# Head-pair loads of B and C turned by VectorE in a chunked scan with a bilinear feed-forward layer

## The chip, the cores and the metric

The kernel runs on one core of a Trainium2 chip. The metric is the device time of one execution in microseconds (us); the median of three runs of the kernel before is 124.91 us (124.63 to 125.03). The core's engines each work through their own list of instructions in order: TensorE (PE in the profile; PEld are its weight loads), VectorE (DVE), ScalarE (ACT), GpSimd (POOL) and SyncE (SP), which here only issues DMAs. SP, ACT and POOL each issue DMAs from their own queue.

## The reference

The inputs are `x` (4 batches, 8 heads, 768 tokens, 32 channels), decays `a` (4, 8, 768), `B` and `C` (4, 8, 768, 16) and three weight matrices, all float32. Per batch and head a linear recurrence is run in chunks:

```python
cum = np.cumsum(log(a)); L = exp(cum_i - cum_j) * causal
y_intra = (C @ B.T * L) @ x                  # inside the chunk
y_inter = (C @ state) * exp(cum)             # from the chunks before
state   = exp(cum_last) * state + sum_j exp(cum_last - cum_j) * B_j x_j
```

Its output, with the 8 heads side by side (3072 rows of 256), goes through `(y @ W_a) * (y @ W_b) @ W_out`, with an inner width of 1536. The result is 3072 x 256 float32.

## The kernel before, in words

The 768 tokens are cut into 6 blocks of 128 tokens, and the 4 batches into 2 pairs of batches, so there are 12 "pairs" p = 2 * block + batch pair. Pairs 0 to 3 (blocks 0 and 1) have an early path of their own, in which two tokens share a partition row. The change leaves that path alone, but for the order of some steps. For pairs 4 to 11 the steps are:

- **Loads.** `loads_bc(p)` issues one DMA for C and one for B of the pair (`load2`, line 163): a partition is a token, and its 256 numbers are 2 batches x 8 heads x 16. So each of the 2048 runs of a DMA is 64 bytes long. `loads_x` does the same for x, with runs of 128 bytes. Nearly all go through SP's queue.
- **Factors.** The decays are scanned on VectorE (`scan`) with the 32 batch-head rows on partitions. `late_rows` (line 276, POOL) divides blocks 2 to 5 by their middle value, into `Ps`; `late_factors` (line 282) turns `Ps` with four 32-row VectorE transposes, so that tokens are on partitions (`fCl`); `fb(k)` takes the reciprocal of one block (`fBl`).
- **Scaling.** `scale_bc` (line 307, POOL) multiplies the loaded B and C with these factors and writes fp16 tiles `bm` and `cm`. `scale_x` (POOL or ScalarE) writes `x16`. `prep(p)` calls the first for C and B.
- **Transposes.** `transposes(p)` (line 323) turns `bm` and `cm` on TensorE, two 128x128 pieces each, into one PSUM bank called `tr`. ScalarE copies from there: twice for B (`bt`, once with the even and once with the odd heads zeroed by `par`) and once for C (`ct`, line 355).
- **Scores.** `scores(p)` (line 366) makes 16 products of `bt` and `ct` into the four banks `SC`; `mask` multiplies three of the four with the causal mask on VectorE, and the fourth either on VectorE too or, `by_pool`, by a ScalarE copy to `tmp` and a POOL multiplication. The results are `t1`.
- **Outputs.** `group(blk)` calls `outputs(blk)` (line 512): products of `ct` with the state, of `x16` with `t1`, and the sums for the next state, `DS`. From PSUM the outputs are read in three parts into `XB`: all of batch 0 of each pair by ScalarE, the two halves of batch 1 by VectorE. `state_sums` (VectorE) and `state_spread` (POOL, writing `spair` and `gU`) update the state.
- **Feed-forward.** `unit(p, k)` for pairs 0 to 3 and `bunit(blk, k)` for blocks 2 to 5 make the two up-products into PSUM banks `aps` and `bps`. ScalarE copies `aps` (`evac_a`), VectorE multiplies it with `bps` into `hk` or `hkb`. `out_half` and `bout` make the down-product into a bank `ops`, which ScalarE copies out and SP stores.

The order on every engine is written out by hand: the calls at the end of the kernel (lines 757 to 1049) are issued in program order, so that block k's scan steps lie between the feed-forward units of block k - 1. Four PSUM banks serve `aps`, `bps`, `ops` and `tr` by turns; which one a product takes is a digit of the string `BANKS` (line 22), and it waits until the bank's last reader is done.

Of the kernel before, what the change touches and what calls it, by code (L numbers as in the profile page):

```python
# [10 lines left out]
f32 = mybir.dt.float32  # L11
# [10 lines left out]
BANKS = (  # L22
    "1301302130213023120312031023120312031203210230123012302103210320132013210231023103201231"
    "0231023102301320132013201321032103210321032103210321032130213021302130213021302130213021"
    "3021302"
)
# [3 lines left out]
def kernel(  # L30
# [26 lines left out]
    NG = NBLK - 1  # L57
    P0 = 4


# [30 lines left out]
    XB = big.tile([128, NBLK - P0 // NBP, 2, 2, NBP, Q], f16, name="XB")  # L91
    U32 = big.tile([128, NP, 2, 2 * D], f32, name="U32")
    gU = big.tile([128, NP, 2, 2 * D], f32, name="gU")
    maskbd = big.tile([128, H, D], f16, name="maskbd")
# [11 lines left out]
    fBl = big.tile([128, NL, NBP * 2 * H], f32, name="fBl")  # L106
    fCl = big.tile([128, NL, NBP * 2 * H], f32, name="fCl")
    hr = big.tile([BH, NG], f32, name="hr")
    hs = big.tile([BH, NG], f32, name="hs")
# [8 lines left out]
    outp = ctx.enter_context(tc.tile_pool(name="outp", bufs=2 * P0 + 2))  # L118
    ps4 = ctx.enter_context(tc.tile_pool(name="ps4", bufs=1, space=PSUM))
    psf = ctx.enter_context(tc.tile_pool(name="psf", bufs=1, space=PSUM))  # L120

# [13 lines left out]


    def tiles(p):
        Bn = inp.tile([128, H, 2, N], f32, name="bn", tag="bn")
        Cn = inp.tile([128, H, 2, N], f32, name="cn", tag="cn")
        Xn = inp.tile([128, H, 2, D], f32, name="xn", tag="xn")  # L140
        pair_in[p] = (Bn, Cn, Xn)
# [17 lines left out]
    def load2(eng, p, which):  # L159
        if p < P0:  # L160
            return [load1(eng, p, which, bt) for bt in range(2)]
        blk, bp = divmod(p, NBP)
        return eng.dma_start(
            by_token(pair_in[p][which]).rearrange("p t h n -> p (t h) n"),
            (B, C, x)[which][2 * bp : 2 * bp + 2, :, blk * Q : (blk + 1) * Q, :].rearrange("t h q n -> q (t h) n"),
        )

    def load_w(W, t, f=None):
# [32 lines left out]
    nc.vector.memset(causal_q, 1.0)  # L201
    nc.vector.memset(c32, 0.0)
    x1 = load1(nc.sync, 1, 2, 0)
    nc.sync.dma_start(c32[0:BH], p32_t.ap())
# [71 lines left out]
    def late_rows(eng):  # L276
# [3 lines left out]
        )  # L280

    def late_factors():
        for c0 in range(0, Q, 32):
            nc.vector.transpose(fCl[c0 : c0 + 32], Ps[:, :, c0 : c0 + 32])

    st = {}
# [20 lines left out]
    def scale_bc(p, which, eng, factor=None):  # L307
        blk, bp = divmod(p, NBP)
        name = ("bm", "cm")[which]
        if p >= P0:  # L310
            f = (fBl, fCl)[which][:, blk - P0 // NBP].rearrange("p (b t h) -> p b t h", b=NBP, t=2)[:, bp]
        else:
            f = (f_c(blk) if which else fB[:, blk])[:, :, bp]
        raw = by_token(pair_in[p][which]) if p >= P0 else pair_in[p][which].rearrange("p h r n -> p r h n")
        m_ = pre.tile([128, 2, H, N], f16, name=name, tag=name)
        eng.tensor_tensor(
            out=m_,
            in0=raw,
            in1=(f if factor is None else factor).unsqueeze(3).broadcast_to((128, 2, H, N)),
            op=ALU.mult,  # L320
        )
        st.setdefault(p, {})[name] = m_
    def transposes(p, ps=None, between=None, apart=False):
        s = st[p]
        if p >= P0:
            ps = [bank("tr").bitcast(f16)] * 2
            TB, TC = ps[0][:, 0:256], ps[0][:, 256:512]
            on_dve = False
        elif ps is None:
            ps = [bank("tb") if p == 1 else SC[0], SC[1]] if apart else None  # L330
            on_dve = apart
            TB, TC = (TT[:, 0:256], TT[:, 256:512]) if ps is None else [t_.bitcast(f16)[:, 0:256] for t_ in ps]
        else:
            on_dve = True
            TB, TC = [t_.bitcast(f16)[:, 0:256] for t_ in ps]
        BT = mid.tile([128, 2, 2, 2, 64], f16, name="bt", tag="bt")
        CT = mid.tile([128, 2, Q], f16, name="ct", tag="ct")
        b_ = []
# [8 lines left out]

        turn(TB, s["bm"])
        if between:
            between()  # L350
        turn(TC, s["cm"])
        copy_bt(0)
        copy_bt(1)
        if p >= P0:
            nc.scalar.copy(CT.rearrange("p t q -> p (t q)"), TC)
            s["BT"], s["CT"] = BT.rearrange("p e r t i -> p e r (t i)"), CT
            return
# [154 lines left out]
    def outputs(blk):  # L512
# [25 lines left out]
        if blk < NBLK - 1:  # L538
            for p in pairs:
                state_sums(p, (1,))  # L540
        whole, low, high = slice(0, 128), slice(0, 64), slice(64, 128)
        for bt, to, fr in ((0, whole, whole), (1, low, high), (1, high, low)):
            if blk == NBLK - 1:
                for j in range(NBP):
                    o_ = XB[to, blk - P0 // NBP, :, bt, j]
                    i_ = SCt[bt][fr, :, cols[j]]
                    if bt == 0:
                        nc.vector.tensor_scalar(o_, i_, YS / XS, None, ALU.mult)
                    else:
                        nc.scalar.activation(out=o_, in_=i_, func=AF.Copy, scale=YS / XS)  # L550
                continue
            o_ = XB[to, blk - P0 // NBP, :, bt].rearrange("p u j q -> p u (j q)")
            i_ = SCt[bt][fr, :, 0 : NBP * Q]
            if bt == 0:
                nc.scalar.activation(out=o_, in_=i_, func=AF.Copy, scale=YS / XS)
            else:
                nc.vector.tensor_scalar(o_, i_, YS / XS, None, ALU.mult)

# [12 lines left out]
    def state_sums(p, bts=(0, 1)):  # L571
        blk, bp = divmod(p, NBP)
        for bt in bts:
# [4 lines left out]
            else:  # L578
                nc.vector.scalar_tensor_tensor(  # L579
                    out=U32[:, p, bt], in0=ds, scalar=g, op0=ALU.mult, in1=gU[:, p, bt], op1=ALU.add  # L580
                )

    def state_spread(p):
# [17 lines left out]
        if blk + 1 < NG:  # L601
            nc.gpsimd.tensor_tensor(
                out=gU[:, p + NBP],
                in0=U32[:, p],
# [128 lines left out]
    def loads_bc(p, eng=None):  # L733
        if p < NP:
            tiles(p)
            for w in (1, 0):
                load2(eng or nc.sync, p, w)

# [4 lines left out]
    def fb(k):  # L743
        if k * NBP >= P0:
            nc.vector.reciprocal(fBl[:, k - P0 // NBP], fCl[:, k - P0 // NBP])
        else:
# [65 lines left out]
    scan(5, NBLK)  # L812
    over_mid(2, NBLK)
    for w in range(2):
        for bt in range(2):
# [67 lines left out]
    scale_bc(3, 1, nc.gpsimd)  # L883
    late_rows(nc.gpsimd)
    scale_x(3, nc.gpsimd)
    pull(2)
    pv(2)
# [5 lines left out]
    h()  # L893
    late_factors()
    fb(2)
    h = unit(2, 1)

    def prep(p, spread=()):
        if p < NP:
            scale_bc(p, 1, nc.gpsimd)  # L900
            scale_bc(p, 0, nc.gpsimd)
        for q in spread:
# [36 lines left out]

    scores(3)  # L940
    prep(4, (2,))
    loads_x(4, nc.sync)
    for p in range(6, NP):
        loads_bc(p)
        if p < 10:
            loads_x(p - 1, nc.sync)
    mask(product(3, 3), by_pool=True)
    mask(product(3, 0))
# [6 lines left out]
    pull(3)  # L955
    pv(3)
    go((2, 5))
    transposes(4)
    state_sums(3)
    state_spread(3)  # L960
    fb(3)
    out_half(2, 0)
# [3 lines left out]
    scores(4)  # L966
    mask(product(4, 3), by_pool=True)
    prep(6)
    masked(4, (0, 1))
# [3 lines left out]
    mask(product(5, 3), by_pool=True)  # L973
    prep_x(5)
    out_half(2, 1)
# [7 lines left out]
    h()  # L983
    go((3, 5))
    group(2)
    transposes(6)
# [4 lines left out]
    stage(6, True, (4, 5))  # L991
    fb(4)
    prep_x(7)
    masked(6, (0, 1))
    masked(6, (2,), *bu(2, 0, 1, 2))
    scale_x(6, nc.scalar)
    bgo(2, 3, 4)
    stage(7, True)
    fb(5)
    prep(8)  # L1000
    prep(9)
    prep_x(8)
    prep(10)
    for p in range(9, NP):
        loads_x(p)
    masked(7, (0, 1, 2), *bu(2, 5, 6, 7, 8, 9, 10, 11))
    group(3)
    transposes(8)
# [7 lines left out]
    masked(8, (0, 1))  # L1016
    masked(8, (2,), *bu(3, 0, 1, 2, 3, 4, 5))
    for blk in range(4, NBLK):
        pB = blk * NBP + 1
        stage(pB, False)  # L1020
        if blk + 1 < NBLK:
            transposes(pB + 1)
        if blk > 4:
            prep_x(pB)
        masked(pB, (0, 1))
        bout(blk - 2, 2)
        masked(pB, (2, 3), *bu(blk - 1, 6, 7, 8, 9))
        group(blk)
        bout(blk - 2, 3)
        bgo(blk - 1, 10, 11)  # L1030
        if blk + 1 < NBLK:
            stage(pB + 1, False, (pB - 1, pB))
            prep_x(pB + 1)
            masked(pB + 1, (0, 1))
            bout(blk - 1, 0)
            masked(pB + 1, (2,))
            transposes(pB + 2)
            bout(blk - 1, 1)
            masked(pB + 1, (3,), *bu(blk, 0, 1, 2, 3, 4, 5))
    last = NBLK - 1  # L1040
# [39 lines left out]
```

## Time and profile before

| what | value |
|---|---|
| median of the runs | 124.91 us |
| the profiled execution's own time | 125.11 us |
| its span in the profile | 123.4 us |
| PE busy | 117.3 us, 95% |
| DVE busy | 91.0 us, 74% |
| ACT busy | 75.7 us, 61% |
| POOL busy | 61.2 us, 50% |
| SP's queue issuing loads | 21.6 to 59.3 us, without a break |
| q1 (SP's and ScalarE's DMAs): packets, share of 16 DMA engines | 51,808, 36.3% |

The profile is of one execution. Times in its timelines count from the start of the span. A line such as `L342 PE MATMUL tr<-ident,bm ... x16 | 2.2, 221 | 0.0` is a group: source line, engine, operation, written tile and read tiles, shapes, number; then busy us in all, mean ns of one; then the idle time of the engine just before these instructions, and what ended it. Matmuls overlap in a pipeline, so what one adds to the path is read from the starts of its neighbours, not from its own length. The granted TensorE clock was full in this execution.

### The profile page before, as it was taken

How to read it: one execution, taken by the hardware profiler on the slowest of the kernel's cores; microseconds unless marked ns; L12 is line 12 of the kernel's file. 1: busy time of each engine (PE TensorE's matmuls, PEld its weight loads, DVE VectorE, ACT ScalarE, POOL GpSimd, SP SyncE). 2: the span in 40 equal slices, each digit the busy share in tenths (PEclk: the TensorE clock that was granted, in tenths of full speed). 3: DMA queues.
4: the chain of work that ended last, by engine and by line, in shares of the span. 5: the costliest groups of instructions: out<-in, count | busy, mean ns of one | idle time of the engine just before them, and what ended most of it. 6: DMA issues, size and time to landing. Idle time of an engine off the chain costs nothing.

```text
span 123.4 us, 3704 instructions
## 1 busy us (share of the span) xinstructions
PE 117.3 (95%) x1456; PEld 80.0 (65%) x1456; DVE 91.0 (74%) x182; ACT 75.7 (61%) x158; POOL 61.2 (50%) x88
## 2 busy tenths in 40 slices
PE   6799799999999999999999999999999999999990
PEld 2345669889898798744477465757464775555890
DVE  3999598973995979799986988996889544747200
ACT  0447846837669866987669767457637746657220
POOL 7997989099492994097996970056000000000000
PEclk9999999999999999999999999999999999999999
DMA  3999999978899989799977601011101012010122
GB/s 66 195 155 210 185 198 204 164 137 77 89 125 115 108 111 103 91 118 93 129 271 169 204 5 45 5 43 45 43 0 43 5 43 88 0 48 0 43 85 85
DMA packets 56401, 12.15 MB, mean 99 GB/s; under 512 B 51168, under 2 KB 55936, under 8 KB 56384
## 3 DMA queue, kind: packets, MB, share of 16 engines
q1 hardware_dynamic: 51808, 7.43, 36.3%
q0 software_dynamic: 2304, 4.06, 17.4%
q10 hardware_dynamic: 2272, 0.43, 1.8%
q8 instruction: 11, 0.18, 0.6%
q14 instruction: 6, 0.05, 0.1%
HBM read 11.13 MB, written 3.15 MB: 116 GB/s over the span
## 4 chain that ended last, share of the span: by engine, by line
PE 85%; DMA 7%; DVE 5%; issue 1%; ACT 0%; DVEq 0%
PE ops L718 17%; PE aps L693 17%; PE bps L693 16%; PE ops L661 9%; PE aps L615 8%; PE bps L615 7%; DMA Wb<-in_moe_w_b_dram 5%; PE SC L372 2%; PE SC L432 2%; PE tr L342 2%; DMA a_sb<-in_a_dram 2%; DVE hk L646 1%; PE bps L628 1%; PE SC L447 1%; PE SC L522 1%; DVE fC L246 1%
## 5 line engine op out<-in xcount | busy, mean ns | idle before, releaser
L639 ACT COPY asb<-aps 128x512 f32<-128x512 f32 x72 | 41.9, 587 | 16.0 <-PE aps L693 10.4
L703 DVE TENSOR_TENSOR hkb<-bps,asb 128x512 f16<-128x512 f32 x48 | 32.3, 688 | 11.8 <-ACT asb L639 10.4
L693 PE MATMUL aps<-XB,Wa 128*128 128x512 f16 x96 | 28.6, 379 | 0.0
L693 PE MATMUL bps<-XB,Wb 128*128 128x512 f16 x96 | 28.5, 379 | 0.0
L718 PE MATMUL ops<-Wo,hkb 128*128 128x256 f16 (+1 forms) x204 | 22.8, 267 | 0.0
L718 PEld LDWEIGHTS <-hkb 128*128 128x128 f16 x204 | 18.4, 98 | 3.0
L426 DVE TENSOR_TENSOR t<-SC,causal_q 128x512 f16<-128x512 f32 x27 | 17.3, 681 | 2.2 <-PE SC L372 2.2
L646 DVE TENSOR_TENSOR hk<-bps,asb 128x512 f16<-128x512 f32 x24 | 15.6, 681 | 3.5 <-ACT asb L639 2.1
L693 PEld LDWEIGHTS <-Wb 128*128 128x128 f16 x96 | 9.9, 103 | 11.0 <-issue 0.2
L693 PEld LDWEIGHTS <-Wa 128*128 128x128 f16 x96 | 9.7, 104 | 9.2 <-issue 0.3
L730 ACT ACTIVATE osb<-ops 128x256 f32<-128x256 f32 (+1 forms) x16 | 6.0, 376 | 12.7 <-PE ops L718 12.6
L615 PE MATMUL bps<-X2T,Wb 128*128 128x256 f16 x84 | 12.6, 273 | 0.1
L615 PE MATMUL aps<-X2T,Wa 128*128 128x256 f16 x84 | 12.5, 273 | 0.2 <-DVE hk L646 0.2
L305 POOL TENSOR_SCALAR x<-xn 128x512 f16<-128x512 f32 x8 | 11.9, 1489 | 0.7
L661 PE MATMUL ops<-Wo,hk 128*128 128x256 f16 x96 | 11.7, 273 | 0.0
L661 PEld LDWEIGHTS <-hk 128*128 128x128 f16 x96 | 9.0, 98 | 1.2
L615 PEld LDWEIGHTS <-Wb 128*128 128x128 f16 x84 | 8.5, 103 | 1.1 <-issue 0.5
L615 PEld LDWEIGHTS <-Wa 128*128 128x128 f16 x84 | 8.4, 104 | 1.2 <-issue 0.5
L424 POOL TENSOR_TENSOR t<-tmp,causal_q 128x512 f16<-128x512 f32 x5 | 5.8, 1156 | 6.2 <-ACT tmp L423 6.1
L426 DVE TENSOR_TENSOR t<-SC,causal 128x512 f16<-128x512 f32 x13 | 8.2, 678 | 0.3 <-PE SC L387 0.2
L595 POOL TENSOR_TENSOR spair<-U,ch 128x128 f16<-128x128 f32 x8 | 3.1, 398 | 10.3 <-DVE U L579 10.3
L346 ACT ACTIVATE bt<-tr,ch 128x256 f16<-128x256 f16 x16 | 6.7, 472 | 0.5 <-PE tr L342 0.5
(101 smaller groups left out, 136.1 us busy)
## 6 DMA issues: line engine op xcount, KB each, us to landing
out_dram<-osb SPq DMA_DIRECT2D x23, 128.0 KB, 1.8
xn<-in_x_dram SPq DMA_DIRECT2D x5, 256.0 KB, 4.6
cn<-in_C_dram SPq DMA_DIRECT2D x8, 128.0 KB, 4.3
bn<-in_B_dram SPq DMA_DIRECT2D x8, 128.0 KB, 4.7
Wo<-in_moe_w_out_dram POOLq DMA_DIRECT2D x2, 384.0 KB, 5.9
xn<-in_x_dram POOLq DMA_DIRECT2D x3, 256.0 KB, 4.8
Wa<-in_moe_w_a_dram POOLq DMA_DIRECT2D x2, 192.0 KB, 5.5
xn<-in_x_dram SPq DMA_DIRECT2D x3, 128.0 KB, 3.5
```

What stands on the lines that cost most here:

```text
L305: eng.tensor_scalar(xo, xi, XS, None, ALU.mult)
L346: b_.append(nc.scalar.activation(out=o_, in_=TB, func=AF.Copy, scale=par[:, e : e + 1]))
L424: nc.gpsimd.tensor_tensor(out=o_, in0=tmp, in1=c_, op=ALU.mult)
L426: nc.vector.tensor_tensor(out=o_, in0=i_, in1=c_, op=ALU.mult)
L615: nc.tensor.matmul(ps[:, kk * 2 * Q : (kk + 1) * 2 * Q], w_up(W, k, f), X2T[:, p, :, f], start=(f == 0), stop=(f == 1), skip_group_check=True,
L639: (nc.vector.tensor_copy if on_dve else nc.scalar.copy)(asb, a_ps)
L646: nc.vector.tensor_tensor(out=s["hk"][:, 2 * k2 : 2 * k2 + 2, :].rearrange("p k q -> p (k q)"), in0=b_ps, in1=asb, op=ALU.mult)
L661: nc.tensor.matmul(o_ps[:, 0:d_model], hk[:, k, bt * Q : (bt + 1) * Q], Wo[:, k, :], start=(k == 0), stop=(k == NK - 1), skip_group_check= ...
L693: nc.tensor.matmul(t_, w_up(W, k, f), XB[:, blk - P0 // NBP, f].rearrange("p t j q -> p (t j q)"), start=(f == 0), stop=(f == 1), skip_gro ...
L703: return lambda: nc.vector.tensor_tensor(out=s["hk"][:, k], in0=ps[1], in1=asb, op=ALU.mult)
L718: nc.tensor.matmul(o_ps[:, 0:w], hk[:, k, c * Q : (c + 1) * Q], Wo[:, k, cs], start=(k == 0), stop=(k == NK - 1), skip_group_check=True,)
L730: nc.scalar.activation(out=o_sb[:, 0:w], in_=o_ps[:, 0:w], func=AF.Copy, scale=1.0 / (YS * YS))
```

## The change

B and C are loaded and turned in another way for the late pairs: C of blocks 3, 4 and 5 (pairs 6 to 11) and B of block 5 (pairs 10 and 11).

- **Loads by head pairs.** `load_block` loads a whole block (both batch pairs) into a tile `rq` with eight DMAs, one per head. A partition now stands for four neighbouring tokens of one pair of heads, 32 partitions per pair of heads, so that a run is 4 x 16 numbers, 256 bytes.
- **Scaling by block.** `scale_block` multiplies the 512 columns of a block in one POOL instruction into `mq`, of which there are two buffers. `prep` calls it for the first pair of the block only.
- **Turning on VectorE.** `turn_pair` transposes 32x32 blocks of `mq` for one pair and writes them as `tq`, token order restored by a step of four elements in the write. For C, `tq` is used directly as `CT`; for B, ScalarE's two `bt` copies read it. TensorE's transposes of these, the `tr` bank of pairs 10 and 11, and ScalarE's `ct` copies of pairs 6 to 11 are gone.
- **Factors by way of DRAM.** For the new layout the factor rows must lie with head pairs on partition groups: `spread_rows` writes the last three blocks of `Ps` to a DRAM tile and reads it back with four DMAs into `Pq`, all on SP; `block_factors` transposes `Pq` into `fCq`, and `last_factors` takes the reciprocal for B of block 5. `late_rows` moves to VectorE, just after the scans, and `late_factors` ahead of pair 2's outputs; `fb(2)` now takes the reciprocal for three blocks at once.
- **Output reads.** In blocks 2 and 3 the second half of batch 1 is read by ScalarE instead of VectorE, and is declared independent of the first half's read.
- **Masks.** The fourth mask of pairs 9, 10 and 11 goes by ScalarE and POOL instead of VectorE.
- **Order and buffers.** Some steps are moved: pair 3's fourth mask ahead of `prep(4)`, `prep_x(5)` ahead of `prep(6)`, x of pair 5 ahead of the loads of block 3, x of pairs 9 to 11 ahead of `prep(10)` on POOL. `gU` gets four slots in place of one per pair, input tiles have fewer buffers, and `BANKS` is a new string.

```diff
+    NT = 3
+    def by_block(blk, which):
+        return blk >= NBLK - NT and (which == 1 or blk == NBLK - 1)
+    def load_block(eng, blk, which):
+        raw = inp.tile([128, nb, 2, 4, N], f32, name="rq", tag="rq", bufs=3)
+        st[("raw", blk, which)] = raw
+        for m, e in itertools.product(range(4), range(2)):
+            eng.dma_start(
+                raw[32 * m : 32 * m + 32, :, e].rearrange("i b g n -> i b (g n)"),
+                (B, C)[which][:, 2 * m + e, blk * Q : (blk + 1) * Q, :].rearrange("b (i g) n -> i b (g n)", g=4),
+            )
+    def scale_block(blk, which, eng):
+        f = fCq[:, blk - (NBLK - NT), :, 0 : 2 * nb] if which else fBq
+        m_ = pre.tile([128, 4, nb, 2, N], f16, name="mq", tag="mq", bufs=2)
+        eng.tensor_tensor(
+            out=m_.rearrange("p g b e n -> p (b e) g n"),
+            in0=st[("raw", blk, which)].rearrange("p b e g n -> p (b e) g n"),
+            in1=f.rearrange("p g j -> p j g").unsqueeze(3).broadcast_to((128, 2 * nb, 4, N)),
+            op=ALU.mult,
+        )
+    def turn_pair(p, which):
+        t_ = mid.tile([128, 2, Q], f16, name="tq", tag="tq", bufs=6)
+        nc.vector.transpose(
+            t_.rearrange("p t (i g) -> p g t i", g=4),
+            st[("scaled", blk, which)][:, :, 2 * bp : 2 * bp + 2].rearrange("p g t e n -> p g t (e n)"),
+        )
+    nc.vector.memset(Pq, 0.0)
+    def last_factors():
+        nc.vector.reciprocal(fBq, fCq[:, NT - 1, :, 0 : 2 * nb])
+    def spread_rows(eng):
+        rows = far.tile([BH, NT, Q], f32, name="rows")
+        eng.dma_start(rows, Ps[:, NL - NT :])
+        for m in range(4):
+            eng.dma_start(Pq[32 * m : 32 * m + 2 * nb], rows.rearrange(...)[:, 2 * m : 2 * m + 2])
+    def block_factors():
+        nc.vector.transpose(fCq..., Pq.rearrange("p k (i g) -> p k g i", g=4))
...
-            nc.vector.reciprocal(fBl[:, k - P0 // NBP], fCl[:, k - P0 // NBP])
+            nc.vector.reciprocal(fBl[:, 0 : NL - 1], fCl[:, 0 : NL - 1])
...
-            if bt == 0:
+            if bt == 0 or (blk < NBLK - 2 and to is high):
...
     over_mid(2, NBLK)
+    late_rows(nc.vector)
+    spread_rows(nc.sync)
...
-    late_rows(nc.gpsimd)
     scale_x(3, nc.gpsimd)
+    late_factors()
+    fb(2)
     pull(2)
     pv(2)
...
     pv(3)
+    block_factors()
     go((2, 5))
...
+    prep_x(5)
     prep(6)
...
     go((3, 5))
+    turn_pair(6, 1)
     group(2)
...
     scale_x(6, nc.scalar)
+    turn_pair(7, 1)
     bgo(2, 3, 4)
...
     masked(7, (0, 1, 2), *bu(2, 5, 6, 7, 8, 9, 10, 11))
+    turn_pair(8, 1)
     group(3)
...
-    masked(8, (2,), *bu(3, 0, 1, 2, 3, 4, 5))
+    masked(8, (2,), *bu(3, 0, 1, 2))
+    turn_pair(9, 1)
+    bgo(3, 3, 4, 5)
     for blk in range(4, NBLK):
-        stage(pB, False)
+        stage(pB, True)
...
         masked(pB, (0, 1))
+        if blk + 1 < NBLK:
+            turn_pair(pB + 1, 0)
         bout(blk - 2, 2)
-        masked(pB, (2, 3), *bu(blk - 1, 6, 7, 8, 9))
+        masked(pB, (2,), *bu(blk - 1, 6, 7))
+        if blk + 1 < NBLK:
+            turn_pair(pB + 1, 1)
+        bgo(blk - 1, 8, 9)
+        if blk + 1 < NBLK:
+            transposes(pB + 1)
         group(blk)
```

## The prediction

> **What bounds the kernel now.** I read the page's busy shares first, then the chain that ended last in order of time, then the timeline of each engine.
>
> ```profile
> PE 117.3 (95%) x1456; PEld 80.0 (65%) x1456; DVE 91.0 (74%) x182; ACT 75.7 (61%) x158; POOL 61.2 (50%) x88
> PE 85%; DMA 7%; DVE 5%; issue 1%; ACT 0%; DVEq 0%
> ```
>
> TensorE is busy 95% of the span and is 85% of the chain. After 13.1 us (the last weight load) the chain leaves it at two places only. Start and length of pieces of the chain:
>
> ```profile
> 15.05 0.69 DVE hk L646
> ...
> 16.12 0.69 DVE hk L646
> 16.85 0.60 PE aps L615 x4
> ...
> 59.50 0.48 DVE t L426
> 60.09 0.69 DVE hkb L703
> 60.83 0.59 PE aps L693 x2
> ...
> 72.81 0.33 PE tr L342 x4
> 73.13 1.31 PE ops L718 x12
> ...
> 82.06 0.33 PE SC L372 x16
> 82.39 1.42 PE ops L718 x12
> ```
>
> At 16.85 and 60.83 a matmul waited until VectorE had emptied its PSUM bank. Elsewhere TensorE runs on, so what leaves its queue leaves the end, unless a new wait takes its place. The last four lines price a transpose: with four (`tr`) the next product starts 0.32 us after them and lasts 1.31; without, it follows the scores and lasts 1.42. Four transposes cost 0.33 + 1.31 - 1.42 = 0.22 us, one 0.055.
>
> **The change part by part.**
>
> *Transposes.* (Line 342.) The order of TensorE's instructions is as before except that 16 transposes go: two each for pairs 6 to 9 (C), four each for pairs 10 and 11 (B and C). 16 x 0.055 = 0.88 us, all on the path.
>
> *PSUM banks.* The bank string is new. Two reuses matter. At 16.85 the W_a product of unit (1,1) waited for VectorE's `hk` that ended at 16.81; it now takes the bank of unit (1,0)'s W_a product, which ScalarE copies from 15.85 to 16.44. TensorE is free at about 16.5, so 0.3 us go; but the W_b product of unit (1,3) now follows a VectorE `hk` and may wait 0.05 to 0.1. I take -0.25, between 0 and -0.35. At 76.01 a pair of L693 lasted 0.53 instead of 0.43, for `hkb` of VectorE; that product now follows a ScalarE copy: -0.10. The wait at 60.83 (0.2) stays.
>
> *VectorE.* Added: eight turns of 128x256 f16. The rows of the same instruction, and one copy that writes with a step:
>
> ```profile
> L284 DVE STREAM_TRANSPOSE fCl<-Ps 32x128 f32<-32x128 f32 x4 | 1.2, 299 | 0.0
> L246 DVE STREAM_TRANSPOSE fC<-Pe 32x64 f32<-32x64 f32 x4 | 0.9, 235 | 0.1
> L358 DVE COPY ct<-SC 128x256 f16<-128x256 f16 x3 | 1.3, 442 | 1.5 <-PE SC L342 1.5
> ```
>
> 64 more elements cost 64 ns, so 256 come to 0.43 and `block_factors` (384) to 0.56. Lower end 0.30, as for 128; upper end 0.69, as VectorE's 512-element rows. I take 0.44, the copy's length at the same shape and type, which writes 4 bytes apart; the turn writes 8 bytes apart. [...]
>
> Also added: `late_rows` from POOL (1.03 there; some 0.65 here), at 13.8, in the 1.25 us that VectorE waited for `bps` before 15.05: covered; were that cover gone, 0.65 at 15.05. The memset of `Pq` (some 0.4) lies in the 1.19 us before the scan at 2.98. The four transposes of `late_factors` (1.24) and the reciprocal over three blocks (0.7, from 0.334 for 32 and 0.253 for 16 columns) move ahead of `state_sums(2)`, which waited 1.48 us there: it starts some 0.4 later, and POOL reads it at 33.9. `block_factors` waits for the rows from DRAM (below); behind it stands `hk` of unit (2,5), which had 0.82 us of idle time ahead of it. Gone: one of four reciprocals of 0.35 (the others are the 0.7 and `last_factors`), two `XB` halves of 0.69, three masks of 0.68. Net about +1.4 us on an engine at 74%.
>
> Where a turn could delay TensorE: the one of pair 7 stands between `hkb` of units 2 and 3 of block 2. There VectorE had 0.27 us idle before unit 3 and some 0.2 before unit 4, so 0.44 fits and 0.69 would be 0.2 late, straight into the wait at 60.83. The turns of pairs 6 and 8 delay the sums that free the score banks: these end at 50.2 and 65.6, needed at 50.9 and 66.5.
>
> *ScalarE.* Six copies of 0.38 go; two `XB` halves (0.60) and three `tmp` copies (0.59) come. The halves stand ahead of `bt` of pairs 6 and 8, which end at about 50.4 and 65.8 for the same two needs. The `tmp` copies fall into waits for `ops` of 0.8 to 1.6 us. Nothing on the path.
>
> *POOL.* Four `scale_block` multiplications, three masks more, `Ps` and eight scales of 0.62 fewer: +2.1 us at 50% busy. Pair 3's mask now stands ahead of pair 4's scales, which end at 35.0 instead of 33.9 and are read at 37.5; the three x loads (3.5) stand ahead of the last two `scale_block`, whose data have landed by then. But POOL runs in order, and two of its results have a date. Engine, start and length:
>
> ```profile
> 39.97 1.49 POOL L305 TENSOR_SCALAR x<-xn 128x512 f16<-128x512 f32 x1
> 41.54 1.16 POOL L424 TENSOR_TENSOR t<-tmp,causal_q 128x512 f16<-128x512 f32 x1
> ```
> ```profile
> 47.30 0.63 PE L432 MATMUL SC<-t,x 128*32 128x128 f16 x32
> 78.17 0.63 PE L432 MATMUL SC<-t,x 128*32 128x128 f16 x32
> ```
>
> First date, block 2: after the mask that starts at 41.54 come x of pair 5 (1.49), `scale_block` of block 3, `bm` of pair 6 (0.62) and the mask of pair 5. A `scale_block` has 512 elements: 1.16 by L424, 1.49 by L305, and I take 1.16, the same operation. The mask then ends at 47.1; the 27th of the 32 matmuls reads it at 47.67. Margin 0.5.
>
> Second date, block 4: the `mq` tiles have two buffers, so `scale_block` of B waits until VectorE has turned pair 9, behind it POOL's whole queue. Counted from the start of the scores of pair 8 (66.74 before): turn ends +4.5, `scale_block` +5.65, mask of pair 8 +6.8, four state products of 0.36 +8.2, x of pair 9 +9.8, mask of pair 9 +11.1. TensorE reads that at +11.5 (78.54, less 0.32 that go in between). Margin 0.4; turns of 0.69 take 0.25 of it, a `scale_block` of 1.49 0.33.
>
> *Loads.* Eight issues of 128 KB become 32 of 32 KB (256-byte runs in place of 64) on SP, and five small ones for the rows' way through DRAM. SP's queue:
>
> ```profile
> 2.65 0.45 SPq L190 DMA_DIRECT2D ch<-ph  x1
> ...
> 21.63 1.28 SPq L154 DMA_DIRECT2D bn<-in_B_dram  x2
> ...
> 33.30 2.03 SPq L163 DMA_DIRECT2D cn<-in_C_dram  x1
> ```
>
> The rows' write can go at 14.5 and its reads end near 21, within the 15.1 us that SP waited for W_out; VectorE reads `Pq` at 36.5. From 21.6 to 59.3 SP issues without a break. An issue of 128 descriptors took 0.45 (L190), of 512 0.64, of 2048 1.2 to 1.6; I take 0.45, ends 0.40 and 1.29 (C's median). x of pair 5 now goes before block 3: its issue ends at 34.6, block 3's eight at 38.2, B of pair 6 starts there and lands 4.7 us later, at 42.9; POOL wants it at 45.35. 16,384 packets of 64 bytes become 4,096 of 256, on a queue whose packets took 13.8 ns each (36.3% of 16 engines over 123.4 us, by 51,808), so landings should rather come earlier. Cost nothing, cover 2.4 us.
>
> *Sum*, against the profiled execution of 125.11 us (span 123.4, 1.7 around it): -0.88 - 0.25 - 0.10 = -1.23, so 123.88. The median of the runs is 124.91, 0.20 lower: 123.68, say 123.7.
>
> **The rivals.**
> 1. Dear turns and a late POOL. With turns at 0.69 and `scale_block` at 1.49, pair 7 costs 0.2, block 4 0.2, block 2 nothing: 124.1; past its margin a late mask counts one for one. For it: margins of 0.4 and 0.5, and the step of the turn's writes. Against: the nearest rows keep both dates. [...]
> 2. The issues are dearer than 0.45 (slower than before). B of pair 6 stands on SP behind block 3's eight issues, and on POOL ahead of pair 5's mask. Above 0.82 us each ((45.35 + 0.54 - 4.7 - 34.6) / 8) TensorE stops in block 2; above 0.97 the gain is gone. At 1.29 it lands at 49.6, 3.7 late: 127.4. For it: each issue waits for the one eight places earlier, and SP has rows up to 3.27. Against: the long rows carry 16 times the descriptors.
> 3. No gain: TensorE's savings come back as waits for banks under the new string, as at 60.83: 124.9. Against: I followed the reuses of blocks 2 to 5 and only the two above get shorter or longer.
>
> **How the numbers follow.** My sum 0.60, rival 1 0.18, rival 3 0.09, rival 2 0.13. A change under 0.3% (0.37 us) can't be told from none here. Faster: 0.60 + 0.18 and a little of rival 3, 0.79; same 0.08; slower 0.13. The range reaches from 123.3 (all of the 0.35 at 16.85, 0.1 hidden stalls) to 124.5 (rival 1, and of rival 3 a take-back of 0.8), leaving out rival 2 and most of 3.
>
> **What would show it.** PE and PEld at x1440 each and the chain 0.9 shorter by them; no `DVE hk` piece before 16.85; turns near 440 ns; the mask of pair 5 ending before the L432 group of block 2 and that of pair 9 before block 4's; SP's `rq` issues near 0.45. I am wrong if TensorE waits for POOL at L432's successor, or for a turn at the scores.

## The result, and the profile after

The kernel after takes 124.27 us (median of 11 executions, 124.04 to 124.90), the kernel before beside it 124.94 us: ratio 0.9946, 95% interval 0.9926 to 0.9966, so 0.3 to 0.7% faster. Run once more with the last set of experiments it took 123.85 us against 124.77: 0.9914 (0.9882 to 0.9945). The forecast was 123.7 us, range 123.3 to 124.5.

Busy shares and the chain's shares by engine, after:

```profile
PE 117.0 (96%) x1440; PEld 79.5 (65%) x1440; DVE 93.4 (76%) x186; ACT 76.4 (62%) x157; POOL 63.3 (52%) x86
PE 90%; DMA 5%; DVE 1%; issue 1%; ACT 1%; POOL 0%; POOLq 0%
```

Sixteen matmuls are gone, and VectorE, ScalarE and POOL all do a little more. TensorE's share of the chain rose to 90%, but 4 of these points are the matmuls of `warmup` (L267, 4.87 us from 1.00 on): up to 5.9 us the chain of this execution runs through them, that of before through the load of the decays and VectorE. The chain that ended last, in order of time (start, length, piece), answers to the pieces shown of before:

```profile
12.71 0.62 PE bps L700 x4
...
15.41 0.25 PE bps L687
15.66 0.58 issue
16.24 0.49 PE bps L687 x3
16.73 0.44 PE aps L687 x4
...
59.05 0.59 ACT asb L711
59.64 0.69 DVE hkb L775
60.37 0.59 PE aps L765 x2
...
71.82 0.33 PE SC L440 x16
72.15 1.42 PE ops L790 x12
```

Three things are to be seen. The four transposes between scores and outputs at 72 are gone: 0.33 and 1.42 follow each other, which were 0.33, 0.33 and 1.31 before. The wait for VectorE's `hkb` (59.64) is still there. And the `hk` pieces ahead of unit (1,1) have gone, but in their place the chain has "issue": TensorE stood in the middle of unit (1,0) for 0.58 us and waited for nothing that the profile shows. (A piece of the chain begins where the one before it ends, and matmuls overlap: the first matmul of unit (1,1) itself starts at 16.57, not at 16.73.)

That last point makes the early part differ from execution to execution, so I cut the time at two places: the start of W_b's first product (12.71 above) and unit (1,1)'s first product (line 615 before, 687 after). The same kernel's second profile (from the last set, "after again") and the profile of before:

| stretch, us | before | after | after again |
| --- | --- | --- | --- |
| start of W_b's first product | 13.12 | 12.71 | 12.88 |
| from there to unit (1,1)'s first product | 3.73 | 3.86 | 3.36 |
| from there to the start of the last ScalarE copy of an output | 103.73 | 102.87 | 102.87 |
| from there to the end of the span | 2.79 | 2.97 | 2.98 |
| span | 123.4 | 122.4 | 122.1 |

The third row is the change in TensorE's queue: -0.86 us, the same in both executions to 0.01. The second row holds the bank term, and is hidden in the first profile. The first row follows the landing of W_b (at 13.07 in the chain of before, at 12.67 in that of after) and differs between executions of one kernel: over the 14 profiles of this case it lies between 12.3 and 13.9, and the two runs of one kernel, e6 and e6b below, have 13.87 and 12.82.

### The profile page after: what moved, and what is told of

Same layout as the page of the kernel before. It is cut to its first block, busy times and chain, and to the rows that moved or that the text cites. A ratio compares the mean times of both kernels' runs of the same rounds, so it can differ in the third digit from the quotient of the medians.

```text
span 122.4 us, 3714 instructions
## 1 busy us (share of the span) xinstructions
PE 117.0 (96%) x1440; PEld 79.5 (65%) x1440; DVE 93.4 (76%) x186; ACT 76.4 (62%) x157; POOL 63.3 (52%) x86
## 4 chain that ended last, share of the span: by engine, by line
PE 90%; DMA 5%; DVE 1%; issue 1%; ACT 1%; POOL 0%; POOLq 0%
PE ops L790 18%; PE aps L765 17%; PE bps L765 16%; PE ops L733 9%; PE aps L687 8%; PE bps L687 8%; DMA Wb<-in_moe_w_b_dram 5%; PE SC L267 4%; PE SC L440 2%; PE SC L500 2%; PE bps L700 1%; PE tr L406 1%; PE SC L515 1%; PE SC L590 1%; PE SC L455 1%
## 5 line engine op out<-in xcount | busy, mean ns | idle before, releaser
L494 DVE TENSOR_TENSOR t<-SC,causal_q 128x512 f16<-128x512 f32 x24 | 15.5, 680 | 3.2 <-PE SC L440 3.2
L492 POOL TENSOR_TENSOR t<-tmp,causal_q 128x512 f16<-128x512 f32 x8 | 9.3, 1159 | 14.5 <-ACT tmp L491 14.3
L687 PE MATMUL bps<-X2T,Wb 128*128 128x256 f16 x84 | 12.6, 272 | 0.6 <-issue 0.6
L491 ACT COPY tmp<-SC 128x512 f32<-128x512 f32 x11 | 6.5, 595 | 1.9 <-PE SC L440 1.1
L267 PE MATMUL SC<-warm 128*128 128x512 f16 (+1 forms) x14 | 5.6, 565 | 1.0 <-POOL warm L238 1.0
```

The lines of the kernel that those rows point to most:

```text
L267: nc.tensor.matmul(bank[:, 0 : 128 * reps], warm, warm.unsqueeze(1).broadcast_to((128, reps, 128)), start=True, stop=True, skip_group_chec ...
L491: nc.scalar.copy(tmp, i_)
L492: nc.gpsimd.tensor_tensor(out=o_, in0=tmp, in1=c_, op=ALU.mult)
L494: nc.vector.tensor_tensor(out=o_, in0=i_, in1=c_, op=ALU.mult)
L687: nc.tensor.matmul(ps[:, kk * 2 * Q : (kk + 1) * 2 * Q], w_up(W, k, f), X2T[:, p, :, f], start=(f == 0), stop=(f == 1), skip_group_check=True,
```

## The experiments

The stretch "unit (1,1) to the last copy" (102.87 in the kernel after) is used below wherever a few tenths matter.

**Sixteen transposes put back on TensorE** (`e1_pe16`).

```diff
         if not by_block(blk, 1):
             turn(TC, s["cm"])
+        elif not by_block(blk, 0):
+            for _ in range(2):
+                turn(TC, s["bm"])
```

> The kernel after, with sixteen more transposes on TensorE: four for each of pairs 6 to 9, of the tile bm, into the half of the tr bank that stands empty; nobody reads them. My theory (what leaves TensorE's queue leaves the end): 16 x 0.055 = 0.88 us come back in full, 0.22 us at each of the four places, so the run takes 0.88 us more than the kernel after and is within 0.2 us of the kernel before (ratio 0.998 to 1.003). Rival: the gain came from elsewhere (the weights' landing, the banks) and the transposes fill idle time of TensorE such as the 0.23 us at 60.37: at most +0.5, so still 0.3 to 0.4% below the kernel before.

Measured: 124.97 us, ratio to before 0.9996 (0.9973 to 1.0018). The stretch is 103.76, +0.89. Its chain, at the first place of block 2:

```profile
47.31 0.44 PE tr L406 x6
47.75 1.31 PE ops L736 x12
```

In the kernel after, two transposes have 0.22 us there:

```profile
47.76 0.22 PE tr L406 x2
47.98 1.31 PE ops L733 x12
```

Matched with the kernel after matmul by matmul, TensorE falls back by 0.21 to 0.23 us at each of the four places where the transposes stand, and nowhere else. So 16 transposes on TensorE are worth 0.89 us of the end, and none of it is absorbed by the wait at 60.

**The bank string, early part** (`e2_banks_early_new`, `e3_banks_early_old`).

```diff
 # e2: before, digits 0 to 45 from after, 46 on renamed 0>1 3>2 2>0 1>3
-    "1301302130213023120312031023120312031203210230...
+    "0123102031203132031023102310213021302130213021...
```

> The kernel before, with only the first 46 digits of the bank string taken from the kernel after (the digits behind them renamed, so that every later reuse stays as it was). My theory: unit (1,1)'s first product then follows ScalarE's copy and starts at about 16.57 in place of 16.85, and what is gained stays: -0.28 us, ratio 0.997 to 0.999, with no hk piece before that product in the chain. Rival: in the kernel after this piece started 0.28 us earlier because Wb had landed 0.41 us earlier and VectorE's hk was earlier with it; the bank alone then gives 0 (ratio 0.9995 to 1.001), because TensorE stops for about 0.5 us inside unit (1,0) in both kernels and the rest of the queue starts from there.

> The kernel after, with the first 46 digits of the bank string taken from the kernel before (those behind them renamed, so that every later reuse stays). If the bank alone made the early gain: +0.28 us against the kernel after, an hk piece before unit (1,1)'s first product. If the earlier hk (its end at about 16.4, before TensorE is through unit (1,0) at 16.57) makes the bank irrelevant: 0, with no such piece.

Measured: e2 125.58 us, ratio 1.0034 (1.0008 to 1.0060), slower than before. e3 (the kernel after with the old digits) 124.06 us, 0.9923 (0.9898 to 0.9949). Both times are at odds with a plain gain of 0.28. The profiles tell why. In e2 unit (1,1) starts 3.37 us after W_b's first product, against 3.73 before: the bank gain is there, and is 0.36. Then nearly twice as much is lost, in this piece of e2's chain:

```profile
31.08 0.69 DVE hk L644
...
31.99 0.30 DVE fCl L282
32.31 0.30 DVE fCl L282
32.62 0.31 DVE fCl L282
...
33.86 0.59 DVE hk L644
```

With the new digits TensorE waits there for a bank that VectorE empties behind the transposes of `late_factors`, which the kernel before has at this place: it falls back by 0.63 us between 34.1 and 35.4. In e3 the start of unit (1,1) is 3.74 behind W_b's product. Its chain has no `hk` piece there, as my second case said, but the timelines of its VectorE and of its TensorE show that VectorE holds the product:

```profile
15.71 1.27 DVE L716 TENSOR_TENSOR hk<-bps,asb 128x512 f16<-128x512 f32 x2
```

```profile
15.90 0.51 PE L685 MATMUL bps<-X2T,Wb 128*128 128x256 f16 x3 [0.26 <-issue]
16.44 0.60 PE L685 MATMUL aps<-X2T,Wa 128*128 128x256 f16 x4
```

The first of the two `hk`, 0.69 long, ends at 16.40; the product follows at 16.44. Without it TensorE would have been there at 16.23: in the kernel after the same product follows 0.33 behind such a restart (16.24 and 16.57). So the old digits hold unit (1,1) at 3.73 to 3.74, in both kernels; the new ones allow 3.36 to 3.38 (e1, e2, e7, e9, e10 and after again; 3.53 in e12, where TensorE came to unit (1,0) 0.16 later). Six executions of e3 don't resolve that 0.37 in the time.

**`late_factors` back in its old place** (`e12_late_factors_back`), to see whether e2's loss belongs to the string or to the order:

```diff
-    late_factors()
-    fb(2)
     pull(2)
...
     h = unit(2, 0, lambda: transposes(3, apart=True))
     h()
+    late_factors()
+    fb(2)
```

> The kernel after, with the four transposes of the late factors and their reciprocal moved back to where the kernel before has them on VectorE, behind unit (2,0)'s product. My theory: the new bank string needs their new place, as the kernel before with the new early digits lost 0.63 us at 34.1 to 35.4, where these instructions stood in its chain: +0.6 to +0.8 us against the kernel after at 32 to 36. Rival: the loss there came of the digits alone: 0.

Measured: 125.20 us, 1.0035 (1.0005 to 1.0065): 1.2% above the kernel after by the ratios of the same set. TensorE falls behind by 0.57 us at 33.8 and by 0.48 at 35.1, 1.05 in all, at the place forecast and somewhat more than forecast. Another 0.5, at 29.8, is not of this edit: this execution was 0.72 early there and met the landing of pair 3's C. The old string under the new order is e3, whose stretch of 102.89 shows no loss. The new string needs VectorE's new order; the loss belongs to the pair of them.

**The turn's price** (`e4_turn_flat`, `e5_turn_twice`).

```diff
 # e4 (and the factor of scale_block is a tile of zeros)
-            t_.rearrange("p t (i g) -> p g t i", g=4),
+            t_.rearrange("p t q -> p (t q)").rearrange("p (g t i) -> p g t i", g=4, t=2),
 # e5
+        for _ in range(2):
             nc.vector.transpose(
```

> The kernel after, with the turns writing 32 neighbouring elements at a time (token order is not restored), and with zeros as the factors of C of blocks 3 to 5 and of B of block 5, so that the scores of the wrong token pairs stay finite: what is computed for these blocks is not the reference's. My theory: the turn's 742 ns come from the write 8 bytes apart, so a turn falls to about 440 ns; VectorE is then 0.3 us earlier in block 2 and the 0.23 us for which TensorE stands at 60.37 go: -0.2 us against the kernel after. Rival: the length comes from the read or from the instruction itself (0.7 us as before) and nothing changes; or the turn is shorter and the stall stays, because it hangs on ScalarE's copies: 0.

> The kernel after, with each of the eight turns done twice (+0.55 us of VectorE each). My theory: the turns are hidden only where VectorE has idle time. Pair 6 and 8: hidden (0.8 and 0.9 us of cover). Pair 7: +0.55 us at 60.37. Pairs 9 and 10: VectorE runs from 66.5 to 84 without a break, so 3 x 0.55 = 1.65 us meet 0.6 us of cover ahead of the scores of pair 10 (81.09), +1.0 us there. Pair 11: mostly hidden. In all +1.5 us against the kernel after, 0.7% above the kernel before. Rival: TensorE waits for banks only, and VectorE at 76% takes 4.4 us more without a loss: 0 to +0.3.

The turns as groups (busy us, mean ns of one, idle before), in the kernel after, in e4 and in e5:

```profile
L202 DVE STREAM_TRANSPOSE tq<-mq 128x256 f16<-128x256 f16 x8 | 5.9, 742 | 0.0
```

```profile
L203 DVE STREAM_TRANSPOSE tq<-mq 128x256 f16<-128x256 f16 x8 | 3.5, 435 | 0.0
```

```profile
L203 DVE STREAM_TRANSPOSE tq<-mq 128x256 f16<-128x256 f16 x16 | 11.9, 747 | 0.3
```

The step of 8 bytes in the write costs 0.31 us of 0.74, the read having been left as it was. The time did not follow: e4 took 124.42 us, 0.9964 (0.9937 to 0.9991), its stretch is 102.95, 0.08 longer than with the dear turns, and the wait at 60 shrank by 0.02. My -0.2 was wrong. Another 0.15 us of the stretch isn't the turn's: B of pair 6 was issued at 43.04 in this execution, 40.80 in the kernel after, and POOL waited for it ahead of pair 5's mask:

```profile
46.52 0.62 POOL L378 TENSOR_TENSOR bm<-bn,fBl 128x256 f16<-128x256 f32 x1 [0.62 <-DMA bn<-in_B_dram]
```

Less that, the flat turns are worth 0.07 us, 0.02 of it at 60. What the shorter turn leaves, VectorE spends waiting for the next product: in the kernel after the two `hkb` behind the turn of pair 7 take 1.30 us, in e4 1.44.

The other direction is not free. e5 took 129.27 us, 1.0348 (1.0306 to 1.0390), where I had expected +1.5. Its stretch is 107.87, +5.0, while VectorE's busy time rose by 6.0 us (93.4 to 99.4). Nearly every turn is paid for: 0.6 us at pair 6's scores and the units behind them, 0.7 ahead of pair 7's scores, 0.5 behind pair 8's, 1.0 at 76, 0.4 ahead of pair 10's scores, 0.9 behind them, 0.8 ahead of pair 11's. A part of its chain in block 2:

```profile
48.93 0.67 DVE tq L203
49.62 0.75 DVE tq L203
...
51.86 0.29 PE SC L441 x8
52.39 0.67 ACT bt L411 x2
53.24 0.62 ACT tmp L492
53.87 0.50 ACT asb L712
54.41 0.60 PE aps L766 x2
```

I had counted 0.8 and 0.9 us of cover for the turns of pairs 6 and 8. But VectorE's idle time there (1.15 us ahead of pair 6's masks in the kernel after) was its wait for scores that themselves wait for VectorE: sums, then scores, then ScalarE's `bt`, `tmp` and `asb`, then the next product. Delay the sums, and the idle time moves along with them.

**Single parts undone** (`e7_xb_dve`, `e9_masks_dve`).

```diff
 # e7 (the two lines that declare the reads independent go too)
-            if bt == 0 or (blk < NBLK - 2 and to is high):
+            if bt == 0:
 # e9: stage(pB, True) and stage(pB + 1, True) become False, masked(pB, (2,), ...) becomes (2, 3), and
-            bgo(blk, 0, 1, 2, 3)
+            masked(pB + 1, (3,), *bu(blk, 0, 1, 2, 3))
```

> The kernel after, with the second half of batch 1 in blocks 2 and 3 read by VectorE again, as in the kernel before. My theory: the sums behind it end 0.62 us later, at about 50.55 and 65.9, and the scores of pairs 6 and 8 need them at 50.71 and 66.13: hidden, 0 (at most +0.1). Rival: the move to ScalarE is what makes room for the turns of pairs 6 and 8, and without it TensorE stands for the sums: +0.4 us at each place.

> The kernel after, with the fourth masks of pairs 9, 10 and 11 on VectorE again, as in the kernel before. My theory, from the run with doubled turns: VectorE runs from 66.5 to 84 without a break there, so the three masks (0.62 us of its time each) no longer fit beside the turns of pairs 9 to 11: +0.6 to +1.5 us against the kernel after, from 76 us on. Rival: POOL and ScalarE lose as much work as VectorE gains, and a fourth mask is not needed before the outputs: 0 to +0.2.

e7: 124.10 us, 0.9949 (0.9926 to 0.9972), stretch 102.88: nothing, as expected; the half read by ScalarE neither helps nor hurts. e9: 124.64 us, 0.9977 (0.9952 to 1.0002), stretch 103.07: +0.20, all of it at 93.4 to 94, in block 4's last units. There my +0.6 to +1.5 fell and the rival's 0 to 0.2 held. The times say more: 0.3% (against the first ratio of the kernel after) to 0.6% or 0.8 us (against the one of the same set). In the profiled execution the rest lies ahead of unit (1,1), where W_b's product starts at 13.39; whether it belongs to the edit isn't shown. The rival's reason, that a fourth mask is needed only at the outputs, fits and was not tested by itself.

**The cover of SP's queue** (`e10_split_block3`).

```diff
+            for b in range(0, nb, 2 if blk == NBLK - NT else nb):
+                bs = slice(b, b + 2 if blk == NBLK - NT else nb)
...
```

> The kernel after, with block 3's eight loads of C cut into sixteen of half the size (same bytes, same runs), to see how far the cover of SP's queue reaches. Each further issue costs 0.43 us (the shortest and commonest length of the eight), so B of pair 6, behind them, is issued and lands 3.4 us later. My theory: the cover worked out in the prediction (2.4 us) is used up and POOL scales B of pair 6 some 1 to 3 us late; pair 5's fourth mask stands behind it on POOL with 0.6 us of margin, and TensorE stops ahead of pair 5's outputs (47.08) for 0.5 to 2.5 us: slower than the kernel after by that much. Rival: issues run ahead of landings (half as many packets each), B of pair 6 still lands in time: 0.

Measured: 128.02 us; the ratio of the three shortest of its six executions is 1.0141 (1.0075 to 1.0207). Two took 126.0 and 126.2 us at a granted clock of 0.997, four 127.8 to 128.5 us at 0.983 to 0.987; all six are above the longest of the kernel after, 124.90. In the profiled one (126.16) the chain runs over SP, then:

```profile
44.28 0.42 SPq L185
44.75 2.78 DMA bn<-in_B_dram
...
47.60 0.62 POOL bm L378
48.22 1.12 POOL t L494
49.38 0.27 PE SC L502 x6
```

B of pair 6 is issued at 44.75 (40.80 in the kernel after), and TensorE's outputs of pair 5 wait for POOL's mask: they go on at 49.38, in the kernel after at 47.36. So 3.95 us of delay cost 2.02, and 1.9 were covered. (TensorE itself lost 1.57 there. It had come 0.45 late, from a wait at 21.6 for POOL's `cm` that the edit doesn't touch.) B was not alone in this. C of the same block, cut up too, also landed late, and POOL scaled it until 47.51, just before it took up B at 47.60:

```profile
46.41 1.10 POOL L193 TENSOR_TENSOR mq<-rq,fCq 128x512 f16<-128x512 f32 x1 [1.97 <-DMA rq<-in_C_dram]
```

Why four executions lost about 2 us more than the profiled one isn't shown.

**A version with the gap used** (`e6_turns_in_gaps`, run twice, and `a_after_again`).

```diff
     group(2)
+    turn_pair(7, 1)
+    last_factors()
...
     scale_x(6, nc.scalar)
-    turn_pair(7, 1)
     bgo(2, 3, 4)
     stage(7, True)
-    last_factors()
```

> The kernel after, with the turn of pair 7 and the reciprocal of block 5's factors moved up on VectorE, to just behind the sums of block 2, where VectorE stood idle for 1.15 us (49.93 to 51.08). My theory: the 0.23 us for which TensorE stands at 60.37 come from VectorE being behind by those 0.55 + 0.26 us, so they go: -0.23 us against the kernel after, and no hkb piece in the chain at 60. Rival: the stall is one of ScalarE's copies and banks (asb before it in the chain), not of VectorE's load: 0. A second rival: the turn, now ahead of the masks of pair 6, delays these (cover left: 0.1 us): +0.1 to +0.2.

> The kernel with the turn of pair 7 and the reciprocal of block 5's factors moved into VectorE's gap, run again beside the kernel after. Theory: TensorE starts units behind 60.4 0.16 us earlier, as in the first profile of it (shift +1.26 ahead of that place, +1.10 behind), so a median 0.1 to 0.2 us below that of the kernel after. Rival: 0.

> The kernel after itself, on the same chip as the other runs of this set. Theory: the start of TensorE's work on W_b (12.7 in its first profile) and its stop inside unit (1,0) differ from execution to execution whatever the kernel; from unit (1,1) on the queue takes the same time as in the first profile to 0.1 us: 0.993 to 0.996 of the kernel before. Rival: the early 0.28 us belong to the kernel: W_b's product again at 12.7 and the stop again until 16.2.

The stall at 60 shrinks from 0.23 us to 0.10 and 0.09. In the chain of the second run no `asb` or `hkb` piece stands there any more:

```profile
59.53 0.43 PE aps L765 x2
59.96 0.43 PE bps L765 x2
60.39 0.52 PE aps L765 x2
```

TensorE gains 0.13 us on the kernel after at that place in the first run and 0.14 in the second. The times don't show it: 124.16 us, 0.9915 (0.9890 to 0.9940), and 124.15 us, 0.9943 (0.9921 to 0.9966), against 0.9946 and 0.9914 for the kernel after itself. It is a version worth keeping on the profile's evidence, and not one that beats the kernel after by measurement. (In its first profile the granted clock was 0.986 over the span, and the first four matmuls of W_b, at 13.87, took 1.04 us, which took 0.62 in the second; only what lies behind them is compared.) Taken with e4, what VectorE owes at 60 is less the turn than the 0.26 us reciprocal of `last_factors`, which stands between pair 7's scores and its masks, with no wait behind it to soak up the change: in this version those masks start about 0.3 us earlier than in the kernel after, in e4 about 0.05, each measured from TensorE's own position. That is argued from the two rows; no run moved the reciprocal alone.

## Why the prediction was right, point by point

- **Transposes, -0.88.** Right, and shown: +0.89 when they are put back, 0.22 for each four.
- **Bank at 16.85, -0.25 (0 to -0.35).** Mechanism right, size too low: 3.73 to 3.36, so -0.37 where nothing else stops TensorE. Two steps were off. The wait of 0.05 to 0.1 taken off for unit (1,3) did not come: TensorE's lead over before stays the same to 0.02 us from unit (1,1) to 48. And "TensorE is free at about 16.5" was true of that execution for a reason that I had not seen. The trace of before has, for the weight loads of that unit:

```profile
15.54 0.10 PEld L615 LDWEIGHTS <-Wb 128*128 128x128 f16 x1
16.17 0.24 PEld L615 LDWEIGHTS <-Wb 128*128 128x128 f16 x3 [0.53 <-issue]
```

  I had read unit (1,0)'s product of 0.89 us as work. Four such matmuls take 0.44 on the chain; the rest was a stop of 0.53 us that ended at 16.17, and 0.33 behind it the next product could start. Without the stop TensorE is free some 0.3 earlier, and ScalarE's copy sets the date. In the first profile of after the stop ended at 16.24, which is 3.53 behind W_b's product (3.05 in before), and hid all of the bank's gain; after again shows it whole:

```profile
15.13 0.45 PE aps L687 x4
15.61 0.59 ACT asb L711
16.24 0.60 PE aps L687 x4
```

  Here unit (1,1) follows ScalarE's copy, as the prediction said it would.
- **Bank at 76, -0.10.** Agrees: TensorE's lead grows by 0.09 us there. The product in the chain, before and after:

```profile
76.60 0.53 PE bps L693 x2
```

```profile
75.72 0.43 PE bps L765 x2
```

- **The wait at 60.83 stays, 0.2.** Right: 0.23 at 60.37.
- **A turn, 0.44 us (0.30 to 0.69).** Mis-sized: 742 ns, above the upper end. 435 ns is what it takes written without the step (e4). The transpose rows of before, 299 ns for 128 elements and 235 for 64, leave 0.17 us beside their slope of 1 ns per element; by that an estimated 1.04 ns per element (265 ns over 256) go to the turn without the step, and 2.23 (572 over 256) to the one with it. So the copy row, which steps 4 bytes and took 442 ns, was the wrong neighbour. `block_factors` took 876 ns in place of 560; it reads 16 bytes apart, which may be the same cost on the read side, but no run changed that read.
- **Rival 1, dear turns cost 0.2 at pair 7 and 0.2 at block 4.** Its first half, the price, came true; its second, the cost, did not: against 435 ns turns TensorE loses 0.02 us at 60 and at most 0.07 in all. `scale_block`, at 1.49 in that rival, took 1.10.
- **POOL's dates, margins of 0.5 and 0.4.** They held, with 0.5 and 0.1. In the timeline of POOL:

```profile
45.70 1.16 POOL L492 TENSOR_TENSOR t<-tmp,causal_q 128x512 f16<-128x512 f32 x1
...
70.97 1.10 POOL L191 TENSOR_TENSOR mq<-rq,fBq 128x512 f16<-128x512 f32 x1 [3.79 <-DMA out_dram<-osb]
...
76.28 1.16 POOL L492 TENSOR_TENSOR t<-tmp,causal_q 128x512 f16<-128x512 f32 x1
```

  The masks end at 46.86 and 77.44; the 27th matmuls of the outputs, which read them, start at 47.36 and 77.55. The 3.79 us wait is the one forecast for the second buffer of `mq`: the turn of pair 9 ends at 70.84. (The releaser named, a store, is the profile's inference.)
- **An issue of SP, 0.45.** Right for most of them, 431 ns at the median. In the view of the tile `rq` (ns, min/median/max):

```profile
L183 SPq DMA_DIRECT2D rq<-in_C_dram x24: 429/431/1612, 35.8 to 60.1; - x24
```

  Eight take 4.9 to 5.9 us for C, 0.61 to 0.74 each, since the first of each eight takes 1.55 to 1.61 and one more 1.38; what holds them, no row says. So the cover of 2.4 us, which decided rival 2, was smaller. Block 3's eight began at 35.83, where I had 34.6, and B of pair 6 was issued at 40.80, where I had 38.2: with the 4.7 us that I gave its landing, POOL would have waited. It did not wait, because B landed sooner (2.8 us after the issue in e10, 3.5 in e4, at most 4.3 here). What TensorE still had was 1.9 us by e10 and 1.3 by e4 (issue 2.24 later, outputs 0.95 later). Rival 2 is a real mechanism, and this change stops short of it by less than I had worked out.
- **`late_factors` moved ahead.** I priced it as a harmless 0.4 us delay of the sums. It is a condition of the new string: in its old place it costs 1.05.
- **Output halves and masks, nothing on the path.** Right for the halves (e7). The masks are worth 0.20 behind unit (1,1) (e9), which the prediction did not count.
- **The sum.** -0.86 behind unit (1,1) in place of -0.98 (the rest are losses of 0.02 to 0.03 at five places), -0.37 ahead of it in place of -0.25, and +0.18 behind the start of the last copy. There SP waits for semaphores one by one, 0.06 us apart: behind the landing of the last store stand four such waits, where before has one (rows of line 1167 and, before, 1075). No part of the prediction has that. It makes -1.05, against -1.23, in an execution without the early stop, and -0.55 in one with it, from the start of W_b's product on. The medians, -0.67 and -0.92, lie between. The direction rests on the transposes. That the missing tenths are the stop's is argued: how often the executions without a profile had it is not known. And there is luck in the range: its room above 123.7 was meant for rivals 1 and 3, and what used it, the stop and the longer end, was in neither.

## What to carry to other kernels

Where TensorE is busy 95% of the span, price a removed step by the starts of its neighbours (here 0.055 us a transpose, 0.89 us for the sixteen of e1), and look at the weight loads as well as the matmuls for idle time before a wait is put down to a bank (0.53 us before 16.17 here). Idle time on another engine is cover only if its end does not depend on the work that is put into it; idle time that waits for TensorE, which waits for the same engine, moves along (in e5 6.0 us more of VectorE cost 5.0). A new order of PSUM banks and a new order of the engine that empties them are one change: the new string without the new order made this kernel slower (e12, 125.20 us and 1.2% above the kernel after, and e2 with its early digits, 125.58 us and 1.0034 of before).

## What was not expected of the hardware

TensorE's stop inside unit (1,0) is plain in six of the 14 profiles, always behind the first or second weight load of the same product, 0.26 to 1.67 us long by the matmuls (in before by the weight loads alone, 0.53). It ends 2.3 to 2.5 us after a packet on a queue that the profile calls "instruction". In the kernel after, the DMA view for 13.9 to 14.0 us has

```profile
q8 instruction: 1, 0.02, 59.2%
```

and the packet starts at 13.98; TensorE resumed at 16.24. The other five pairs are 13.78 and 16.17 (before), 13.49 and 15.90 (e3), 14.57 and 17.05 (e4), 14.87 and 17.33 (e5), 13.80 and 16.24 (e6, second run). A seventh, short one is in e10 and ends at 15.97:

```profile
15.97 0.21 PEld L689 LDWEIGHTS <-Wb 128*128 128x128 f16 x2 [0.20 <-issue]
```

Where the packet came at 12.6 or 12.9 (e1, e7, e12), TensorE did not stop. In 12 profiles (all but e10 and the first of e6, for which no view gives the packet) the third weight load of this product starts 2.3 us or more after the packet, and the stop is what is missing to that when TensorE gets there. Over the whole span of the kernel after the page counts 11 packets and 0.18 MB on this queue; what they carry, no view says. That the packet causes the stop is argued from these times; no run moved it on purpose, and what sets its own time, while the weights are landing, stays open.
